# Retention attention and ELU FFN in one kernel: w_out staged and cast by GpSimd, first FFN1 tiles beside the last unit, the tail of batch 0 behind batch 1's units

## The chip, the cores and the metric

The kernel runs on one core of one Trainium2 chip. The metric is the device time of one execution in microseconds; a kernel is timed in several executions beside runs of the kernel before on the same chip. Each run comes with its span and its mean granted TensorE clock and is called fast or slow. PE is the matrix engine, PEld its weight load, DVE VectorE, ACT ScalarE, POOL GpSimd, SP SyncE, whose queue issues most transfers.

## The reference

```python
# q, k, v: (8, 8, 576, 64) fp32;  w_in: (512, 2048), w_out: (2048, 512) fp32
scores = scale * q @ k.T                       # per batch and head
D = gamma[h] ** (i - j)  where i >= j, else 0
x = ((scores * D) @ v)                         # -> (4608 tokens, 512)
h = x @ w_in
g = where(h > 0, h, exp(min(h, 0)) - 1)        # ELU
out = g @ w_out                                # (4608, 512) fp32
```

## The kernel before

A "unit" is a piece of attention: two 128-token chunks of four heads, or a tail of 64 tokens of all heads. A batch has four units and a tail, so units 0 to 3 and tail 4 are batch 0, units 5 to 8 and tail 9 batch 1. A unit is loaded in fp32, multiplied by decay factors into bf16 ("cast"), transposed (early units on PE, later ones by DMA), and then its matmuls run (`stretch`). The running state of a head group goes through `s_mid` and `s_end`, both made on GpSimd. The FFN works on blocks of 256 tokens: FFN1 tile (block, f) makes `ph`, the ELU makes `g`, FFN2 adds up in `pm`. All instructions are pinned: each engine runs its own in the order of the program.

Names in the lines below: `rqk`, `rv` are loaded q/k and v, `qkn`, `vn` their casts (`rqt`, `qkt`, `rvt`, `vt` for a tail), `ptr` a tile transposed on PE and `qkT` its copy (its "eviction") that the unit's matmuls read; `x`, `xt` are the attention result and its bf16 copy; `e` and `em` are exp(h) and exp(h) - 1 of the ELU; `ot` is the output copied out of `pm`. FT is 4 and NU is 5. Fillers are matmuls on zeros that only keep PE busy.

```python
def load_out(n):                               # w_out: cast fp32 -> bf16 in the transfer
    f = slice(n * 4, n * 4 + 4)
    pin(nc.gpsimd.dma_start(w_out_sb[:, f], moe_w_out.rearrange(...)[:, f]))

def cast(u, q="p", v="p"):                     # a full unit
    if q:
        cast_q(u, nc.vector if q == "v" else nc.gpsimd)   # two multiplies of q
        cast_q(u, nc.gpsimd, 1)                           # two multiplies of k
    if v:
        cast_v(u, v)

def stretch(u, quick=False):                   # cut: conditions
    new_x(); inter(u - 1); scores(u); values(u - 1); state(u)
    prefix_mid(u); put_mid(u)                  # DVE; POOL: s_mid
    masks(u)                                   # DVE, 1.2 us
    put_x(u - 1)                               # ACT
    prefix_end(u); put_end(u)                  # DVE; POOL: s_end

# ... end of the first stage
for ft in range(8, 16):
    ffn2(0, 0, [ft]); ffn2(0, 1, [ft], ps_x, "x0")
    if ft == 9:  cast(FT); cast(FT + 1, "v", "s")
    if ft == 11: load_to(FT + 7)
    if ft == 13: cast(FT + 2, "v", "s")
# second stage: q = FFN2 group of block 1, t = transposes, u = unit, f = FFN1 tile of block 2
for what in "q t q u t q u7 q t q u8 t q q u f t q f u f f t f9 u f f f".replace(" ", ""):
    if what == "7":   cast(FT + 3, "v", "s")
    elif what == "8": cast(FT + 4, "v", "s"); cast(FT + 5)
    elif what == "9": cast_later(FT + 6); cast_later(FT + 7); load_to(FT + 8)
    else: ...          # do it; after an "f" also chore(2): two pending casts
# main loop: FFN1 of block k beside FFN2 of block k - 1, a unit every few tiles
```

## Time and profile before

| | before |
|---|---|
| median (3 runs) | 326.02 us (325.49 to 326.57) |
| span of the profiled run | 324.5 us, clock 0.989 |
| end of the first FFN2 (last pm matmul before the ot copies) | 46.28 us |
| main loop starts (FFN1 tile (3,0)) | 72.11 us |
| last matmul ends | 319.68 us |

The last rows are read from the PE timeline. From 72 us on PE is full, so I read the kernel as a prologue and a main loop of 247.6 us (PE busy 243.5). The prediction below shows the lines.

### The profile page before, as it was taken

How to read it: one execution, taken by the hardware profiler on the slowest of the kernel's cores; microseconds unless marked ns; L12 is line 12 of the kernel's file. 1: busy time of each engine (PE TensorE's matmuls, PEld its weight loads, DVE VectorE, ACT ScalarE, POOL GpSimd, SP SyncE). 2: the span in 40 equal slices, each digit the busy share in tenths (PEclk: the TensorE clock that was granted, in tenths of full speed). 3: DMA queues.
4: the chain of work that ended last, by engine and by line, in shares of the span. 5: the costliest groups of instructions: out<-in, count | busy, mean ns of one | idle time of the engine just before them, and what ended most of it. 6: DMA issues, size and time to landing. Idle time of an engine off the chain costs nothing.

```text
span 324.5 us, 8896 instructions
## 1 busy us (share of the span) xinstructions
PE 304.5 (94%) x3566; PEld 205.8 (63%) x3610; DVE 205.9 (63%) x357; ACT 180.2 (56%) x352; POOL 168.1 (52%) x292
## 2 busy tenths in 40 slices
PE   7888989879899999999999999999999999999983
PEld 2347746666666676666676666667666667666641
DVE  3837756677577677667776767568666766555430
ACT  3527655585555565555665555655565555654531
POOL 5962414596777676846664857664593722010000
PEclk9959999999999999999999999999999999999999
DMA  7999999439999957966568496837685410001102
GB/s 208 259 177 205 229 274 222 120 67 259 260 211 200 229 133 161 228 162 162 149 164 203 107 245 151 171 119 188 157 148 130 73 45 35 32 34 48 49 33 66
DMA packets 99373, 49.60 MB, mean 153 GB/s; under 512 B 43588, under 2 KB 96836, under 8 KB 99332
## 3 DMA queue, kind: packets, MB, share of 16 engines
q1 hardware_dynamic: 92436, 36.19, 50.7%
q0 software_dynamic: 6896, 12.85, 16.5%
q8 instruction: 28, 0.46, 0.6%
q14 instruction: 13, 0.11, 0.1%
HBM read 36.70 MB, written 9.44 MB: 142 GB/s over the span
## 4 chain that ended last, share of the span: by engine, by line
PE 79%; DMA 7%; ACT 4%; DVE 3%; POOL 3%; issue 2%; SPq 1%; DVEq 0%; ACTq 0%; POOLq 0%
PE ph L65 35%; PE pm L65 35%; PE x L65 5%; PE sc L65 3%; DMA w_out_sb<-in_moe_w_out_dram 3%; DMA qkT<-qkn 2%; DMA rqk<-in_k_dram 2%; POOL qkn L186 1%; DVE g L505 1%; DVE g L509 1%; ACT xt L355 1%; ACT e L502 1%; ACT ot L520 1%; ACT ph L504 1%; SPq L175 1%
## 5 line engine op out<-in xcount | busy, mean ns | idle before, releaser
L65 PE MATMUL pm<-w_out_sb,g 128*128 128x512 bf16 x534 | 139.2, 379 | 4.1 <-ACT ot L520 1.7
L65 PE MATMUL ph<-xt,w_in_sb 128*128 128x256 bf16 x1024 | 134.0, 275 | 4.6 <-DVE g L509 2.3
L65 PEld LDWEIGHTS <-w_in_sb 128*128 128x128 bf16 x1152 | 110.5, 98 | 41.0 <-issue 6.1
L502 ACT ACTIVATE e<-ph 128x512 f32<-128x512 f32 x144 | 85.8, 597 | 88.6 <-PE ph L65 88.5
L65 PEld LDWEIGHTS <-g 128*128 128x128 bf16 x576 | 55.9, 98 | 44.5 <-issue 3.1
L505 DVE SCALAR_TENSOR_TENSOR g<-e,ph 128x512 bf16<-128x512 f32 x72 | 49.4, 686 | 43.4 <-ACT ph L504 42.3
L508 DVE TENSOR_SCALAR em<-e 128x512 bf16<-128x512 f32 x72 | 40.7, 565 | 33.3 <-ACT e L502 33.3
L381 POOL TENSOR_TENSOR s_mid<-mid,diag 128x256 bf16<-128x256 f32 x32 | 19.5, 611 | 75.3 <-DVE mid L390 39.6
L509 DVE SCALAR_TENSOR_TENSOR g<-ph,em 128x512 bf16<-128x512 f32 x72 | 49.8, 692 | 8.2 <-PE ph L65 0.9
L186 POOL TENSOR_TENSOR qkn<-rqk,gk 128x256 bf16<-128x256 f32 x64 | 40.6, 650 | 9.7 <-DMA rqk<-in_k_dram 9.5
L504 ACT ACTIVATE ph<-ph 128x512 f32<-128x512 f32 x72 | 42.7, 593 | 0.0
L536 POOL DMA_DIRECT2D out_dram<-ot x31 | 17.7, 573 | 40.0 <-ACT ot L520 39.9
L306 DVE TENSOR_TENSOR pt<-sc,mask 128x1024 bf16<-128x1024 f32 x31 | 37.7, 1216 | 0.4 <-PE sc L65 0.4
L355 ACT CAST xt<-x 128x256 bf16<-128x256 f32 x62 | 23.5, 450 | 24.5 <-PE x L65 20.5
L186 POOL TENSOR_TENSOR qkn<-rqk,gq 128x256 bf16<-128x256 f32 x48 | 30.8, 656 | 0.1
L520 ACT COPY ot<-pm 128x512 f32<-128x512 f32 x36 | 21.2, 590 | 7.0 <-PE pm L65 7.0
L381 POOL TENSOR_TENSOR s_end<-end,diag 128x256 bf16<-128x256 f32 x32 | 22.2, 696 | 2.1 <-DVE end L397 2.1
L65 PE MATMUL sc<-qkT 64*64 64x128 bf16 (+1 forms) x576 | 16.0, 220 | 1.4 <-DMA qkT<-qkn 0.8
L65 PE MATMUL ph<-xtt,w_in_sb 128*128 128x256 bf16 x128 | 16.6, 273 | 0.1
L231 POOL CAST vn<-rv 128x512 bf16<-128x512 f32 x25 | 16.2, 647 | 0.0
L65 PEld LDWEIGHTS <-qkT 64*64 64x64 bf16 x576 | 9.9, 106 | 6.7 <-ACT qkT L256 2.7
L256 ACT COPY qkT<-ptr 128x512 bf16<-128x512 bf16 x16 | 9.1, 596 | 8.3 <-PE ptr L255 8.3
(69 smaller groups left out, 166.8 us busy)
## 6 DMA issues: line engine op xcount, KB each, us to landing
rqk<-in_q_dram SPq DMA_DIRECT2D x32, 256.0 KB, 4.4
rqk<-in_k_dram SPq DMA_DIRECT2D x32, 256.0 KB, 4.2
rv<-in_v_dram SPq DMA_DIRECT2D x32, 256.0 KB, 5.0
out_dram<-ot POOLq DMA_DIRECT2D x31, 256.0 KB, 3.3
w_in_sb<-in_moe_w_in_dram POOLq DMA_DIRECT2D x4, 512.0 KB, 7.4
w_out_sb<-in_moe_w_out_dram POOLq DMA_DIRECT2D x4, 512.0 KB, 9.4
rqt<-in_q_dram SPq DMA_DIRECT2D x8, 128.0 KB, 3.8
rqt<-in_k_dram SPq DMA_DIRECT2D x8, 128.0 KB, 3.9
```

The lines of the kernel that those rows point to most:

```text
L65: pin(nc.tensor.matmul(*a, **kw))
L186: pin(eng.tensor_tensor(natt[u][0][:, i, e], x[:, e], g[:, e], ALU.mult))
L306: pin(nc.vector.tensor_tensor(pt.rearrange("p i h n -> p (i h) n"), sc.rearrange("p i (h n) -> p (i h) n", h=2), mask.rearrange("p k e r - ...
L355: pin(engines[eng[c]](dst.rearrange("p h (r e) -> p h e r", e=2), src))
L381: pin(eng.tensor_tensor(dst.rearrange("p h (j d) -> p h j d", j=2), src.unsqueeze(2).to_broadcast([P, 2, 2, D]), diag.unsqueeze(1).unsquee ...
L502: pin(nc.scalar.activation(e, ph, AF.Exp))
L504: pin(nc.scalar.activation(ph, ph, AF.Relu))
L505: pin(nc.vector.scalar_tensor_tensor(g, e, -1.0, ph, ALU.add, ALU.min))
L508: pin(nc.vector.tensor_scalar_add(em, e, -1.0))
L509: pin(nc.vector.scalar_tensor_tensor(g, ph, 0.0, em, ALU.max, ALU.min))
L520: pin(nc.scalar.copy(ot, pm))
L536: pin(eng.dma_start(out[r : r + P, :], ot))
```

## The change

Its intent: take the cast of w_out out of its transfers (they become plain loads from SP with casts on GpSimd), let the first FFN1 tiles fill PE while the last unit of batch 0 is prepared, and move tail 4 behind units 5 to 8. The core of the diff, with cuts (some arguments of calls too are cut):

```diff
-    def load_out(n):  # cast in the transfer, from GpSimd
+    def load_out(n):
+        staged[n] = raw.tile(...)
+        for i in range(2):
+            pin(nc.sync.dma_start(staged[n][:, i], moe_w_out[f * P : (f + 1) * P, :]))
+    def cast_out(n, eng="pp"):
+        for i in range(2):
+            pin(engines[eng[i]](w_out_sb[:, 2 * n + i], staged[n][:, i]))
...
+    sequence = [0, 1, 2, 3, 5, 6, 7, 8, 4] + list(range(9, NS))
...
+    turn_pe(3, "sv", 3, st[1])          # three filler matmuls
+    cast_v(3, "s")
+    ph = hidden(0, 0)                   # FFN1 tile (0,0) beside unit 3
...
+    ffn1(1, 0)
+    after(gts[1, 0], nc.sync)           # w_out is released here
+    for n in range(NFT // 2):
+        load_out(n)
+        cast_out(n)
+    load_to(NU + 1)                     # units 5, 6, 7 behind w_out
...
-    for what in "q t q u t q u7 q t q u8 t q q u f t q f u f f t f9 u f f f".replace(" ", ""):
+    for what in "q q q t q u t q u 7 q q t q u 8 f f t f u 4 f t f u 9 f t f u f".replace(" ", ""):
         if what == "7":
-            cast(FT + 3, "v", "s")
+            cast(NU + 2, "p", "s")      # q of unit 7 now on GpSimd
+            load_to(NU + 3)
         elif what == "8":
+            cast(NU + 3, "p", "s")
...
+        elif what == "4":
+            cast(FT)                    # tail of batch 0
+        elif what == "9":
+            cast(NU + FT)
...
+    for u in range(2 * NU, 2 * NU + 3):
+        cast_later(u)                   # units 10, 11, 12: only now
```

More of the change, by code (lines that the diff above doesn't have):

```diff
@@ L123 @@
     s_mid = [const.tile([P, 2, P], BF16, name=f"s_mid{w}") for w in range(2)]
-    s_end = [[const.tile([P, 2, P], BF16, name=f"s_end{w}{t}") for t in range(2)] for w in range(2)]
+    s_end = [[[const.tile([P, 2, P], BF16, name=f"s_end{w}{t}{o}") for o in range(2)] for t in range(2)]
+             for w in range(2)]
     diag = const.tile([P, 2], FP32, name="diag")
@@ L135, with load_in @@
     dummy = const.tile([1, 4], FP32, name="dummy")
-    def load_in(n):
-        c = slice(n * 512, (n + 1) * 512)
+    staged = {}
+    def load_in(a, b):
+        c = slice(a * 512, b * 512)
         pin(nc.gpsimd.dma_start(w_in_sb[:, :, c], moe_w_in.rearrange("(j p) c -> p j c", p=P)[:, :, c]))
     def load_out(n):
-        f = slice(n * 4, n * 4 + 4)
-        pin(nc.gpsimd.dma_start(w_out_sb[:, f], moe_w_out.rearrange("(f p) c -> p f c", p=P)[:, f]))
+        staged[n] = raw.tile([P, 2, 4, 2, D], FP32, name="rqk", tag="rqk").rearrange("p i h e d -> p i (h e d)")
+        for i in range(2):
+            f = 2 * n + i
+            pin(nc.sync.dma_start(staged[n][:, i], moe_w_out[f * P : (f + 1) * P, :]))
+    def cast_out(n, eng="pp"):
+        for i in range(2):
+            pin(engines[eng[i]](w_out_sb[:, 2 * n + i], staged[n][:, i]))
     def after(tile, eng):
@@ L244, in turn, with turn_pe @@
             pin(nc.sync.dma_start_transpose(trt[u], flat(u)))
-    def turn_pe(u, eng="vs", between=0):
+    def turn_pe(u, eng="vs", between=0, d=None):
         n = turn_tile(u)
@@ L249, in turn_pe @@
             if i and between:
-                warm(between)
+                warm(between, d)
             if i * 4 < n:
@@ L316, in inter @@
                 o = xps[0][:, hp * ST : (hp + 1) * ST]
-                acc_x(0, 2, o, s_end[hp // 2][1][:, hp % 2], trt[u][:, hp, :ST])
+                acc_x(0, 2, o, s_end[hp // 2][1][b % 2][:, hp % 2], trt[u][:, hp, :ST])
             return
@@ L321, in inter @@
                 continue
-            s = s_mid[w] if c else s_end[w][0]
+            s = s_mid[w] if c else s_end[w][0][b % 2]
             x = (to or xps)[c]
@@ L404, in put_end, with mask_half @@
         b, T, w, tail = unit(u)
-        block_diag(s_end[w][T], total[w])
-    def last_of_start(u, bank):
-        sc = score_ps.pop(u)
-        pt = ppool.tile([P, 2, 2, 2 * P], BF16, name="pt", tag="pt")
-        ptt[u] = pt
-        for hl in range(2):
-            pin(nc.vector.tensor_tensor(
-                pt[:, :, hl], sc.rearrange("p i (h n) -> p i h n", h=2)[:, :, hl],
-                mask.rearrange("p k e r -> p (k e r)").unsqueeze(1).to_broadcast([P, 2, 2 * P]), ALU.mult,
-            ))
-        first = [hidden(0, 0)]
-        for hl in range(2):
-            values(u, (hl,), bank)
-            inter(u, (hl,), bank)
-            put_x(u, (hl,), bank, ("ss", "sv")[hl])
-            if hl == 0:
-                first.append(hidden(0, 1, ps_m, "pm"))
-        drop(u)
-        elu(0, 0, first[0])
-        elu(0, 1, first[1])
+        block_diag(s_end[w][T][b % 2], total[w])
+    def mask_half(u, hl):
+        if hl == 0:
+            ptt[u] = ppool.tile([P, 2, 2, 2 * P], BF16, name="pt", tag="pt")
+        pin(nc.vector.tensor_tensor(
+            ptt[u][:, :, hl], score_ps[u].rearrange("p i (h n) -> p i h n", h=2)[:, :, hl],
+            mask.rearrange("p k e r -> p (k e r)").unsqueeze(1).to_broadcast([P, 2, 2 * P]), ALU.mult,
+        ))
+    before = [None]
     def stretch(u, quick=False):
-        late = u - 1 in natt and u - 1 in ptt
+        p, before[0] = before[0], u
+        late = p is not None
         carry = u < NS and not unit(u)[3]
@@ L433, in stretch @@
         if late:
-            inter(u - 1)
+            inter(p)
         if u < NS:
@@ L437, in stretch @@
         if late:
-            values(u - 1)
+            values(p)
         if carry:
@@ L444, in stretch @@
         if late and not quick:
-            put_x(u - 1)
+            put_x(p)
         if u < NS:
@@ L449, in stretch @@
             if quick:
-                put_x(u - 1)
-            drop(u - 1)
+                put_x(p)
+            drop(p)
         if carry:
@@ L457, in stretch @@
             put_end(u)
-    def finish(u):
-        new_x()
-        inter(u)
-        values(u)
-        put_x(u)
-        drop(u)
     xts, gts, acc = {}, {}, {}
@@ L496, in hidden, with elu, elu_act @@
         return ph
-    def elu(k, f, ph):
-        relu = f % 2 == 1
+    def elu(k, f, ph, relu=None):
+        elu_act(k, f, ph, relu)()
+    def elu_act(k, f, ph, relu=None):
+        relu = f % 2 == 1 if relu is None else relu
         e = epool.tile([P, TG], FP32, name="e", tag="e")
@@ L504, in elu, with rest @@
             pin(nc.scalar.activation(ph, ph, AF.Relu))
-            pin(nc.vector.scalar_tensor_tensor(g, e, -1.0, ph, ALU.add, ALU.min))
-        else:
-            em = epool.tile([P, TG], BF16, name="em", tag="em")
-            pin(nc.vector.tensor_scalar_add(em, e, -1.0))
-            pin(nc.vector.scalar_tensor_tensor(g, ph, 0.0, em, ALU.max, ALU.min))
+        def rest():
+            if relu:
+                pin(nc.vector.scalar_tensor_tensor(g, e, -1.0, ph, ALU.add, ALU.min))
+            else:
+                em = epool.tile([P, TG], BF16, name="em", tag="em")
+                pin(nc.vector.tensor_scalar_add(em, e, -1.0))
+                pin(nc.vector.scalar_tensor_tensor(g, ph, 0.0, em, ALU.max, ALU.min))
+        return rest
     def ffn2(k, it, fts, pool=None, tag="pm"):
@@ L548, with load_to @@
     loaded = [0]
-    def load_to(u):
-        while loaded[0] <= u:
-            load(loaded[0], last=(loaded[0] == FT - 1))
+    sequence = [0, 1, 2, 3, 5, 6, 7, 8, 4] + list(range(9, NS))
+    def load_to(n):
+        while loaded[0] <= min(n, NS - 1):
+            load(sequence[loaded[0]], last=(loaded[0] == FT - 1))
             loaded[0] += 1
@@ L561 @@
     cast(1, "v", None)
-    load_in(0)
+    load_in(0, 1)
     for u in range(FT - 1):
@@ L581 @@
             cast(2, "v", None)
-            load_in(1)
             warm(2, st[1])
@@ L591 @@
             put_end(1)
+            load_in(1, 2)
             cast_q(3, nc.vector)
             cast_q(3, nc.gpsimd, 1)
-            cast_v(3, "p")
-            load_in(2)
-            load_in(3)
             warm(3, st[1])
-    masks(2)
-    turn_pe(3, "vs")
-    st3 = [ps_h.tile([P, TG], FP32, name="st", tag="ph") for _ in range(2)]
-    state(3, st3)
     prefix_mid(2)
@@ L604 @@
     prefix_end(2)
+    load_in(2, 4)
+    masks(2)
+    turn_pe(3, "sv", 3, st[1])
+    cast_v(3, "s")
+    ph = hidden(0, 0)
+    st3 = [ps_h.tile([P, TG], FP32, name="st", tag="ph") for _ in range(2)]
+    state(3, st3)
     prefix_mid(3)
@@ L608 @@
     scores(3)
+    rest = elu_act(0, 0, ph, True)
+    mask_half(3, 0)
+    rest()
+    mask_half(3, 1)
+    ph = hidden(0, 1, ps_m, "pm")
     new_x()
@@ L613 @@
     drop(2)
-    last_of_start(3, st3)
+    elu(0, 1, ph)
     put_end(2)
     put_end(3)
-    load_out(0)
-    after(s_end[0][1].rearrange("p h d -> p (h d)"), nc.sync)
-    load_to(FT + 3)
-    for blk, n in ((1, 0), (0, 1), (1, 1)):
-        ffn1(blk, 2 * n)
-        ffn1(blk, 2 * n + 1)
-        after(gts[blk, 2 * n], nc.gpsimd)
-        load_out({(1, 0): 1, (0, 1): 2, (1, 1): 3}[blk, n])
+    for hl in range(2):
+        values(3, (hl,), st3)
+        inter(3, (hl,), st3)
+        put_x(3, (hl,), st3, ("ss", "sv")[hl])
+        if hl == 0:
+            ffn1(0, 2)
+    drop(3)
+    ffn1(1, 0)
[4 more added lines that the diff above has]
+    load_to(NU + 1)
+    ffn1(0, 3)
+    for f in range(1, 4):
+        ffn1(1, f)
     for n in range(2, 4):
@@ L632 @@
         ffn2(0, 1, [ft], ps_x, "x0")
-        if ft == 9:
-            cast(FT)
-            cast(FT + 1, "v", "s")
-        if ft == 11:
-            load_to(FT + 7)
-        if ft == 13:
-            cast(FT + 2, "v", "s")
-    turns = [lambda u=u: turn_pe(u, "ss") for u in range(FT, NU + FT + 1)]
-    units = [lambda u=u: stretch(u, True) for u in range(FT, NU + FT + 1)]
+    cast(NU, "v", "s")
+    cast(NU + 1, "v", "s")
+    order = sequence[4:10]
+    turns = [lambda u=u: turn_pe(u, "ss") for u in order]
+    units = [lambda u=u: stretch(u, True) for u in order]
     quads = [lambda it=it, part=part: ffn2(1, it, part) for it in range(2) for part in Q]
     tiles = [lambda f=f: ffn1(2, f) for f in range(8)]
-    for what in "q t q u t q u7 q t q u8 t q q u f t q f u f f t f9 u f f f".replace(" ", ""):
+    for what in "q q q t q u t q u 7 q q t q u 8 f f t f u 4 f t f u 9 f t f u f".replace(" ", ""):
         if what == "7":
-            cast(FT + 3, "v", "s")
+            cast(NU + 2, "p", "s")
+            load_to(NU + 3)
         elif what == "8":
-            cast(FT + 4, "v", "s")
-            cast(FT + 5)
+            cast(NU + 3, "p", "s")
+            load_to(NU + 4)
+        elif what == "4":
+            cast(FT)
+            load_to(NU + 5)
         elif what == "9":
-            cast_later(FT + 6)
-            cast_later(FT + 7)
-            load_to(FT + 8)
+            cast(NU + FT)
+            load_to(NU + 6)
         else:
             {"q": quads, "t": turns, "u": units, "f": tiles}[what].pop(0)()
-            if what == "f":
-                chore(2)
     assert not (turns or units or quads or tiles)
-    cast_later(FT + 8)
-    load_to(FT + 10)
     stores()
-    first = FT + 6
+    for u in range(2 * NU, 2 * NU + 3):
+        cast_later(u)
+        load_to(u + 2)
+    first = 2 * NU
     slots = {}
```

## The prediction

> **What bounds the kernel now.** I read the page first, for where the matmul engine is full.
>
> ```profile
> PE   7888989879899999999999999999999999999983
> ...
> PEclk9959999999999999999999999999999999999999
> DMA  7999999439999957966568496837685410001102
> ```
>
> One slice is 8.1 us. From about 72 us to the end PE stands at 9: the rest is the fixed FFN work at full clock and nothing in the diff makes it smaller. Anything to win or lose lies in the first nine slices. There PE has holes, the clock dips in slice 3, and the transfer engines are full for seven slices. The table by stretches puts sizes on this:
>
> ```profile
> 45.60:72.10 26.50, 22.21 (x368) 15.73 (x370) 15.79 (x29) 17.12 (x37) 14.63 (x24) 1.00 0.67 149
> 72.10:100.00 27.90, 26.29 (x347) 18.34 (x352) 20.47 (x33) 15.72 (x31) 19.20 (x33) 1.00 1.13 245
> 0.00:25.26 25.26, 19.74 (x269) 9.65 (x272) 13.21 (x41) 10.04 (x23) 17.47 (x43) 0.86 1.03 213
> ```
>
> The first figure after the stretch's length is PE busy, then PEld, DVE, ACT, POOL, then the clock. PE is idle 5.5 us up to 25.3, and loses 3.3 us more there to a half clock (0.50 from 18.0 to about 24.5: 6.5 us at half speed). From 45.6 to 72.1 it is idle 4.3 us. With 1.5 us between these, some 14.5 us are lost before the main loop starts at 72.1 (first tile of FFN block 3). That is the whole purse: a gain of 2% (6.5 us) must take nearly half of it.
>
> Next, the waits of PE over the whole span and the POOL timeline:
>
> ```profile
> PE ph L65 <- DVE g L509: 2.3, 2, 1.7
> PE ph L65 <- ACT xt L355: 1.8, 3, 0.9
> PE pm L65 <- ACT ot L520: 1.7, 3, 0.8
> ...
> PE pm L65 <- DMA w_out_sb<-in_moe_w_out_dram: 0.4, 1, 0.4
> ```
>
> The w_out transfers, which the chain view charges with 3% (10.85 us), make PE wait only 0.4 us. They land just in time, at 44.4. Taking the cast out of them can give 0.4 us directly.
>
> ```profile
> 51.72 0.61 POOL L381 TENSOR_TENSOR s_mid<-mid,diag 128x256 bf16<-128x256 f32 x1 [6.47 <-DVE mid L390]
> 53.05 0.73 POOL L381 TENSOR_TENSOR s_end<-end,diag 128x256 bf16<-128x256 f32 x1 [0.72 <-DVE end L397]
> 53.74 1.36 POOL L186 TENSOR_TENSOR qkn<-rqk,gk 128x256 bf16<-128x256 f32 x2
> ```
>
> POOL works in program order. Unit 5's state matmuls end at 51.2; s_end is done at 53.8, because DVE's mask (1.2 us) lies between. So a cast written after a unit starts on POOL 2.55 us after that unit's last matmul. Unit 6 shows it again: 54.9 to 57.5. Before, this cost PE nothing, since casts run two units ahead: unit 8's k cast ends at 58.8, its transposes start at 60.3.
>
> **What the Trainium skill says.** "DMA: Bandwidth & Descriptors", Issuing engines are not separate DMA queues: transfers from SP and POOL share the same 16 engines. The trace agrees: the DMA share is 1.06 to 1.24 from 5 to 60 us whichever queue issues, so moving w_out to SP makes no bandwidth. Same page, Rules for kernel authors: a cast during a DMA is issued from GpSimd; so w_out from SP must be cast by an engine. "GPSIMD Engine Reference", 4.1 Engine selection: one-input elementwise work is roughly at line rate on GpSimd, two-input work about 2x slower than on VectorE. Here the 128x512 cast takes 647 ns on POOL, a 128x256 two-input multiply 656 ns, against a median of 426 ns on DVE: 1.5x. "TensorE: Matmul & The Clock Gate", Why this matters for your kernels: PE-idle gaps above about 3 us bring the half clock back. The trace has the half clock at 18 us after a stretch of short matmuls (1.23 us busy in 15 to 17), without a single gap of 3 us; the 1.7 us gap at 65.7 did not cause it.
>
> **The change, part by part.**
>
> (a) *Start, to FFN1 tile (1,0), at 25.26 before.* POOL loses the vn cast of unit 3 (0.6) and gets one w_in issue fewer; tile (0,0) is issued while unit 3 is prepared; three filler matmuls are added. By rows: w_in's first quarter is issued at 9.4 and lands in up to 8.3 us, at 17.7; tile (0,0) at full clock 0.95 to 18.7; state and scores 0.7; tile (0,1) 0.9; unit 2's matmuls 0.9 to 21.2. Then ACT is in the way: xt of unit 2 (0.76), exp and relu of tile 1 (1.1), xt (0.5), exp of tile 2 (0.6), then DVE em, g, xt (1.5): 25.7. So three tiles done by 25.8, where before has two by 25.3 and three by 26.2: gain 0.4 us. The half clock goes (3.3 us), but most of this turns into waiting for that chain.
>
> (b) *w_out to the end of FFN2 of half block 0, at 45.6 before.* SP waits for g of tile (1,0): matmuls to 26.7, exp, em, g about 1.9: 28.6. The dummy transfer takes 0.76 to issue; first 256 KB lands some 2.9 later (the shortest landing of a 256 KB load): 32.3; cast 0.65: 33.0. PE wants it at 31.4 (five tiles from 25.8 at about 1.05, as before's seven took 7.35, and one more): 1.6 us wait. Then 16 slices of 262 KB at 270 to 310 GB/s of what is read (estimates: 20.8 to 44.4 us before carried some 6.4 MB; 5 to 10 us ran at 295) take 0.85 to 0.97 us each, beside a 0.65 us cast that hides. The last is ready at 45.5 to 47.5. FFN2 ends near 46.7: **loss 1.1 us**. The 16 casts (10.4 us of POOL) fill its idle time.
>
> (c) *Second stage, 26.5 us before.* The loads of units 5 to 8 now follow w_out, so k of unit 7 lands about 52.7, and casts run only one unit ahead; q of units 7 and 8 is now on POOL: four multiplies, 2.44 us. Unit 7: two matmul groups (1.75) after unit 6, its transposes come up; POOL is at 2.55 + 2.44 = 5.0, transposes end at 5.3. They take 0.6 themselves, so PE idles 2.95. Unit 8: two FFN tiles follow unit 7 (the known 0.9 xt wait, done at 2.95): idle 1.75. Unit 4, the moved tail: its cast stands behind unit 8's s_end, late by the ELU of the tile before (about 3.3), 1.2 more, one tile (0.9) to cover it: idle 3.5. Unit 9's cast is hidden. With the 0.45 for ot and 0.4 in evictions the stage idles 0.45 + 0.4 + 2.95 + 0.9 + 1.75 + 3.5 = 10 us instead of 4.3: with rounding **loss 5.7 to 7 us**; I take 6.5.
>
> (d) *Main loop.* Before, unit 10's casts were slipped in from "f9" on; now they come after the tail casts and four output issues (2.2): about 12.3 us after unit 8's end, plus some 4.2 for the DMA transpose: 16.5. PE is at unit 10 after 10.5 + 3.5 = 14. Idle 2.2, against 0.8 before at unit 11: loss 1.4. The rest is unchanged.
>
> Sum: -0.4 + 1.1 + 6.5 + 1.4 = +8.6 us: 326.0 + 8.6 = **334.6 us**.
>
> **The rivals.** First, the clock: without the half clock 3.3 us come back in full, w_out at 310 GB/s lands by 44.5, the stalls of (c) are shorter since PE arrives later: about 328 to 330, same. For it: the fillers and early tiles clearly aim there. Against: the ACT chain of (a), each piece of which has a measured row. Second, the clock the other way: stalls of 3 us bring the half clock back in the second stage, 1 to 2 us each: 337 to 341. For it: the dip at 18 us; against: 1.7 us at 65.7 did nothing. Third, transfers become the bound: if w_out runs below 270 GB/s, units 7 and 8 land after POOL could cast them, and (b) and (c) grow by 2 to 4 us. For it: landings of up to 13.5 us under load; against: w_out's rows are 2 KB, units' pieces 512 B. Fourth, a real gain: all waits of (c) hidden and the clock kept, some 320. I see nothing that hides them.
>
> **Range and chances.** 334.5 us. The stalls in (c) follow from program order and measured durations, so a loss is likelier than not; that (a) and (b) give 3 to 4 us more than I count is quite possible. 8 in 10: 328 to 341. The 2% lines are 319.5 and 332.5. Faster 0.06 (half the purse would have to be won), same 0.32, slower 0.62.
>
> **What would show it.** (a) clock 1.00 from 15 to 26, PE waiting for ACT xt near 24 and tile (1,0) at 25.8; (b) first w_out matmul near 33, a wait for a POOL cast there, last near 46.7; (c) PE "ptr" waits for POOL qkn and qkt of about 3, 1.7 and 3.5 us between 55 and 76; (d) main loop starting near 80 and a wait of about 2 us for a qkT transfer just after. The prediction is wrong if the main loop starts at or before 74, which needs POOL's casts ahead of PE, or if the loop itself runs at another rate than its 247.6 us from 72.1 to 319.7.

## The result, and the profile after

The changed kernel takes 338.28 us in the median of four runs (334.36, 339.77, 338.86, 337.7; the second counts as slow, at a clock of 0.971; the median of the three fast ones is 337.7), the kernel before 326.19 us beside it. The ratio is 1.0333, 95% interval 1.0241 to 1.0425: slower. A ratio here is the mean time of one kernel's fast runs over that of the other's of the same rounds, so it isn't quite the ratio of the medians that I quote. The profiled run is the fastest, 334.36 us (span 332.7); what follows is read from it, and it therefore shows 8.2 of the 12.1 us by which the medians differ.

First the same rows of the page, in 40 slices of 8.3 us.

```profile
PE   8778986757999999999999999999999999999994
...
PEclk9999999799999999999999999999999999999999
DMA  7994999927589995895856885856569410000102
```

The clock dip has moved from slice 3 to slice 8, PE is now at 6, 7, 5 and 7 tenths in slices 7 to 10 (9, 8, 7 and 9 before), and the transfer engines now have a hole in the fourth slice, where SP waits to release w_out. The table by stretches (PE, PEld, DVE, ACT, POOL busy, clock, DMA share, GB/s):

```profile
0.00:25.10 25.10, 20.07 (x287) 10.50 (x288) 15.12 (x45) 12.79 (x28) 15.05 (x40) 1.00 0.98 209
25.10:45.00 19.90, 18.31 (x132) 12.72 (x131) 12.37 (x21) 11.22 (x21) 10.13 (x16) 1.00 0.82 265
45.00:79.30 34.30, 24.68 (x368) 15.94 (x368) 14.42 (x26) 18.48 (x37) 19.04 (x33) 0.95 0.90 210
```

The second stage, 25.8 us before (46.28 to 72.11), lasts 34.3 us: PE idles 9.6 us of it, where it idled 4.3 in the prediction's stretch of before. The clock of 0.95 over 34.3 us is another 1.7 us. The PE waits of the whole run:

```profile
PE ptr L264 <- POOL qkn L195: 4.4, 12, 1.3
PE ptr L264 <- POOL qkt L207: 3.1, 2, 2.8
PE ph L65 <- DVE g L508: 2.3, 3, 1.8
PE ph L65 <- ACT xt L364: 1.8, 3, 0.9
PE pm L65 <- POOL w_out_sb L152: 1.4, 1, 1.4
```

The first two are the stalls of step (c), but for 1.2 us of `qkn` waits in the first stage: transposes ("ptr") that wait for multiplies on GpSimd. Here is one transpose before (unit 8, no wait), and the first of unit 7 after:

```profile
60.30 0.61 PE L255 MATMUL ptr<-ident,qkn 128*128 128x128 bf16 x8
57.00 0.28 PE L264 MATMUL ptr<-ident,qkn 128*128 128x128 bf16 x2 [1.26 <-POOL qkn L195]
```

The timelines of PE and POOL around tail 4 show the order that makes the longest one:

```profile
69.02 1.05 PE L65 MATMUL ph<-xt,w_in_sb 128*128 128x256 bf16 x8
72.91 0.28 PE L264 MATMUL ptr<-ident,qkt 128*128 128x128 bf16 x2 [2.84 <-POOL qkt L207]
```

```profile
71.67 0.61 POOL L390 TENSOR_TENSOR s_end<-end,diag 128x256 bf16<-128x256 f32 x1 [0.65 <-DVE end L406]
72.24 1.19 POOL L207 TENSOR_TENSOR qkt<-rqt,gq 128x256 bf16<-128x256 f32 x2
```

POOL was idle before 71.67 and tail 4's data had long landed (its loads were issued by 52.5 us, and no load of a tail takes more than 5.9 us to land); but its cast stands behind unit 8's s_end in the program, and s_end waits for DVE. PE had one tile to do meanwhile.

One thing nobody foretold stands at the start of the main loop (DVE timeline):

```profile
78.56 3.61 DVE L507 TENSOR_SCALAR em<-e 128x512 bf16<-128x512 f32 x1 [0.35 <-ACT e L498]
82.27 0.69 DVE L508 SCALAR_TENSOR_TENSOR g<-ph,em 128x512 bf16<-128x512 f32 x1
```

An em takes 0.46 us in the median; this one took 3.61, and PE waited 1.81 us for its g.

| | before | after | difference |
|---|---|---|---|
| nine FFN1 tiles done | 32.6 | 30.3 | -2.3 |
| end of the first FFN2 | 46.28 | 44.99 | -1.3 |
| main loop starts | 72.11 | 79.3 | +7.2 |
| last matmul ends | 319.68 | 327.97 | +8.3 |

The second stage thus costs 8.5 us, the main loop 1.1 more, and the start had won 1.3.

### The profile page after: what moved, and what is told of

Its sections match the earlier page's. It is cut to its first block, busy times and chain, and to the rows that moved or that the text cites. A ratio compares the mean times of both kernels' runs of the same rounds, so it can differ in the third digit from the quotient of the medians.

```text
span 332.7 us, 8976 instructions
## 1 busy us (share of the span) xinstructions
PE 308.6 (93%) x3613; PEld 205.7 (62%) x3613; DVE 204.9 (62%) x352; ACT 181.8 (55%) x354; POOL 174.8 (53%) x303
## 4 chain that ended last, share of the span: by engine, by line
PE 77%; DMA 7%; POOL 5%; DVE 4%; ACT 3%; SPq 2%; issue 2%; DVEq 0%; POOLq 0%; ACTq 0%
PE pm L65 34%; PE ph L65 34%; PE x L65 5%; PE sc L65 3%; DMA rqk<-in_moe_w_out_dram 3%; POOL qkn L195 2%; DMA rv<-in_v_dram 2%; DMA rqk<-in_k_dram 2%; DVE em L507 1%; SPq L184 1%; ACT e L498 1%; DVE g L508 1%; POOL s_end L390 1%; SPq L148 1%; POOL s_mid L390 1%
## 5 line engine op out<-in xcount | busy, mean ns | idle before, releaser
L65 PE MATMUL pm<-w_out_sb,g 128*128 128x512 bf16 x576 | 147.0, 380 | 2.7 <-POOL w_out_sb L152 1.4
L65 PE MATMUL ph<-xt,w_in_sb 128*128 128x256 bf16 x1024 | 132.6, 273 | 4.7 <-DVE g L508 2.3
L504 DVE SCALAR_TENSOR_TENSOR g<-e,ph 128x512 bf16<-128x512 f32 x73 | 50.2, 687 | 44.6 <-ACT ph L500 43.6
L507 DVE TENSOR_SCALAR em<-e 128x512 bf16<-128x512 f32 x71 | 42.9, 604 | 38.0 <-ACT e L498 38.0
L508 DVE SCALAR_TENSOR_TENSOR g<-ph,em 128x512 bf16<-128x512 f32 x71 | 49.1, 691 | 7.8 <-PE ph L65 0.5
L195 POOL TENSOR_TENSOR qkn<-rqk,gk 128x256 bf16<-128x256 f32 x64 | 39.7, 638 | 7.1 <-DMA rqk<-in_k_dram 6.9
L195 POOL TENSOR_TENSOR qkn<-rqk,gq 128x256 bf16<-128x256 f32 x52 | 33.4, 658 | 0.1
L152 POOL CAST w_out_sb<-rqk 128x512 bf16<-128x512 f32 x16 | 10.1, 641 | 13.0 <-DMA rqk<-in_moe_w_out_dram 12.4
```

Source lines behind the costliest of these rows:

```text
L65: pin(nc.tensor.matmul(*a, **kw))
L195: pin(eng.tensor_tensor(natt[u][0][:, i, e], x[:, e], g[:, e], ALU.mult))
L504: pin(nc.vector.scalar_tensor_tensor(g, e, -1.0, ph, ALU.add, ALU.min))
L507: pin(nc.vector.tensor_scalar_add(em, e, -1.0))
L508: pin(nc.vector.scalar_tensor_tensor(g, ph, 0.0, em, ALU.max, ALU.min))
```

## The experiments

Eleven kernels ran (e2 twice), all with right results.

### e1: q of units 7 and 8 back on VectorE

```diff
-            cast(NU + 2, "p", "s")
+            cast(NU + 2, "v", "s")
-            cast(NU + 3, "p", "s")
+            cast(NU + 3, "v", "s")
```

> The changed kernel with one edit: the q multiplies of units 7 and 8 go to VectorE instead of GpSimd. Theory A (transposes of units 7, 8 and 4 wait because their casts stand on GpSimd behind the preceding unit's s_end): two of four multiplies (1.2 us) leave GpSimd for each of the two units, so the transpose waits on qkn between 55 and 68 us fall from 3.2 us to about 1, the main loop starts some 2.4 us sooner, and the half clock at 57 to 61 us may go too: 334 to 336 against 338. Rival B (the loads behind w_out come too late): same waits, now ended by transfers, 338.

Measured: 331.6, 331.42, 338.2 and 338.62 us (before: 326.35); the last two are slow, at clocks of 0.98. The PE waits from 45 to 85 us have POOL qkn at 0.5 and DVE qkn at 0.8 us instead of POOL qkn at 3.2; the tail's wait (3.1 us) is untouched. The waits go as theory A says, and no transfer took their place; a wait of 1.3 us for a g did, and the half clock only moved, to 71.5 us. The fast runs lie below the 334 to 336 us expected. By how much the time falls is inconclusive: two fast runs, and the changed kernel's own fast runs spread over 4.5 us.

### e2 and e2b: the casts one unit earlier

```diff
-"q q q t q u t q u 7 q q t q u 8 f f t f u 4 f t f u 9 f t f u f"
+"q q q t q u 7 t q u 8 q q t q u 4 f f t f u 9 f t f u f t f u f"
```

> The changed kernel with the casts (and loads) of units 7, 8, 4 and 9 each written one unit earlier, as far ahead as in the kernel before; engines unchanged. Theory A: the transpose waits on qkn and qkt (6.3 us in the second stage) fall below 1 us, the half clock there goes, the second stage shrinks from 34.3 to about 27 us, total 329 to 331. Rival B: GpSimd now waits for the transfers of units 7 and 8 instead, later s_mid and s_end are held up behind them, and less than 2 us are won: 336 or more.

> The same kernel as e2_casts_ahead, whose only profile fell in a run of 1735 us and shows nothing. Theory A, which its times (330 to 331) favoured: in the second stage the transpose waits on GpSimd multiplies stay below 1 us in sum and the clock stays at 1.00; 330 to 331 again. Rival B: waits for transfers in their place.

Measured: 330.85, 330.21, 330.88 us (ratio 1.0137), then 330.28, 327.75, 330.74, 329.45 us on another chip (ratio 1.0089). One run of e2, the profiled one, took 1736 us; I have no explanation for it and read nothing from it, hence e2b. In e2b's PE waits from 45 to 90 us no wait on a GpSimd multiply is left at all; the first lines are

```profile
PE ph L65 <- DVE g L508: 2.8, 2, 2.5
PE ptr L264 <- DVE g L508: 1.1, 1, 1.1
PE ph L65 <- ACT xt L364: 0.9, 1, 0.9
```

So theory A holds: moving the four places where casts and loads are issued, with no work taken away, removes 6.3 us of waits and brings the ratio from 1.0333 to 1.0137 and 1.0089 (the mean of the fast runs from 337 to 330 us). Rival B is out for this order: the data were there. The longest wait left, 2.5 us, is for the g behind a long em again (4.38 us from 72.04 on), and a half clock follows it (0.74 in 75 to 80 us), against the expectation.

### e3: the second stage of before behind the new start and the staging

Against the changed kernel, with cuts:

```diff
-sequence = [0, 1, 2, 3, 5, 6, 7, 8, 4] + list(range(9, NS))
+sequence = list(range(NS))
     for ft in range(8, 16):
...
+        if ft == 9:  cast(FT); cast(FT + 1, "v", "s")
+        if ft == 11: load_to(FT + 7)
+        if ft == 13: cast(FT + 2, "v", "s")
...
-"q q q t q u t q u 7 q q t q u 8 f f t f u 4 f t f u 9 f t f u f"
+"q t q u t q u7 q t q u8 t q q u f t q f u f f t f9 u f f f"     # with before's casts at 7, 8, 9
```

> The changed kernel's start and staged w_out, with the second stage of the kernel before (tail first, its order of tiles, casts two units ahead, early casts for the main loop). Theory A: the whole loss lies in the second stage; that stage takes about 26 us again and the 1.3 us that start and staging had won by the end of the first FFN2 remain: 324 to 326. Rival B (staging moves the loads of units 4 to 7 behind w_out and these then come too late for any order): waits for transfers of 3 us or more after 45 us, 329 or more.

Measured: 334.13 us, ratio 1.0242. Theory A in this form is a miss. The PE timeline shows where the time went:

```profile
44.69 0.59 PE L65 MATMUL pm<-w_out_sb,g 128*128 128x512 bf16 x2 [0.39 <-POOL w_out_sb L152]
52.16 1.86 PE L65 MATMUL pm<-w_out_sb,g 128*128 128x512 bf16 x4 [6.88 <-ACT ot L521]
```

The old stage has v casts on ACT ahead of the ot copies. With the loads of units 4 to 6 behind w_out, ACT waits there for data (6.48 us before the first v cast, 2.04 before the second), and the ot copy behind it:

```profile
51.01 0.62 ACT L240 CAST vn<-rv 128x512 bf16<-128x512 f32 x1 [2.04 <-DMA rv<-in_v_dram]
```

Rival B is right in part: staging on SP does make the units late, and the old order cannot bear it.

### e4: the new start alone

Against e3, with cuts:

```diff
-    after(gts[1, 0], nc.sync)
-    for n in range(NFT // 2):
-        load_out(n)
-        cast_out(n)
+    load_out(0)                          # right after unit 3's s_end, as in before
+    after(s_end[0][1][0], nc.sync)       # (its first row)
+    load_to(FT + 3)
...
+    load_out(1)                          # after tile (1,0); 2 and 3 after two more tiles each
```

> The new start alone (first FFN1 tiles beside unit 3, fillers), with w_out cast in its transfers and the second stage of the kernel before. Theory A: no half clock from 18 to 24 us and tile (1,0) near 24 instead of 25.3 with one more tile done, so about 1.5 to 2 us less: 324 to 325. Rival C (the w_out landing at 44 us sets the end of the first FFN2 whatever comes before it): PE waits 2 us more for w_out, total 326 as before.

Measured: 326.5 us, ratio 1.0026 (interval 0.9975 to 1.0077): same. The time is as rival C said, but not quite for its reason: it named the last w_out landing, at 44 us, and in the profiled run (329.52, the slowest of four) PE waits 2.44 us for the first transfer, at 33 us, and 1.96 us for an ot copy, which stands on ACT behind a v cast that waits for its load:

```profile
33.37 0.59 PE L65 MATMUL pm<-w_out_sb,g 128*128 128x512 bf16 x2 [2.44 <-DMA w_out_sb<-in_moe_w_out_dram]
...
48.51 1.25 PE L65 MATMUL pm<-w_out_sb,g 128*128 128x512 bf16 x4 [1.96 <-ACT ot L515]
```

What the start wins is given back at the next waits. e3 against e4 also shows that staging with the units' loads put behind w_out, under the old order, costs 7.6 us by the medians; the two edits were not run apart.

### e5: the early casts behind the ot copies

Against e3:

```diff
-        if ft == 9:
-            cast(FT); cast(FT + 1, "v", "s")
-        if ft == 11: load_to(FT + 7)
-        if ft == 13: cast(FT + 2, "v", "s")
+    cast(FT); cast(FT + 1, "v", "s"); load_to(FT + 7); cast(FT + 2, "v", "s")
```

> e3_old_second_stage with one edit: the early casts of units 4, 5 and 6 stand behind the two ot copies. In e3 PE waited 6.9 us for an ot copy. Theory D (ScalarE works in program order and the v cast of unit 6, written ahead of the ot copies, waits for its late transfer): the 6.9 us wait becomes under 0.6, total 326 to 328, with a smaller wait for late units after it. Rival B in its strong form (the units come too late for any order): the same 6 us turn up as waits of the transposes or of s_mid, total 332 or more.

Measured: 331.69 us, ratio 1.0155 (e3: 1.0242). The 6.9 us wait for ot becomes 0.7 in sum, as theory D says; but a wait of 3.8 us for a transposed tile's eviction on ACT has taken its place, and the clock is at 0.56 from 50 to 55 us. Between the two theories, and above theory D's 326 to 328: the order on ACT set where the late data hurt, and some 60% of the loss against before (4.7 of 7.8 us) stays.

### e6 and e9: is it the long em?

Tiles of the named blocks use the other ELU form, which has no em:

```diff
-        elu(k, f, hidden(k, f))
+        elu(k, f, hidden(k, f), True if (k, f) in ((2, 6), (3, 0)) else None)                     # e6
+        elu(k, f, hidden(k, f), True if (k, f) in ((2, 4), (2, 6), (3, 0), (3, 2)) else None)     # e9
```

> The changed kernel, where the ELU of two tiles (block 2 tile 6, block 3 tile 0) goes by the relu form, which has no em instruction. In the changed kernel's trace one em lasted 3.61 us instead of 0.43 while GpSimd ran multiplies without a break, and PE waited 1.81 us for it at the start of the main loop. Theory E (em cannot get at SBUF while GpSimd reads and writes it; the other forms can): no VectorE instruction over 1.5 us between 74 and 90 us, and that wait is gone or under 0.5 us. Rival F (VectorE is slow there for any instruction, or em waited for its input): the relu form's g is stretched likewise and the wait stays.

> The changed kernel with tiles 4 and 6 of block 2 and 0 and 2 of block 3 in the relu form, so that no em stands beside GpSimd's unbroken stretch of work from 70 to 84 us. In e6, with two such tiles, the em before them took the stall: 5.84 us from 74.3 on. Theory E (em cannot get at SBUF until GpSimd leaves a gap): no VectorE instruction above 1.5 us between 68 and 90 us, no PE wait on g above 0.6 us there, 1.8 to 4 us less than the changed kernel: 333 to 336. Rival F (VectorE stalls there whatever it runs): another instruction is stretched to several us and the time stays at 334 to 339.

e6 ran once, 339.43 us at a clock of 0.978 (a single run, state unknown). It missed its aim in a telling way: the em of the tile before, untouched by the edit, met the same work on POOL.

```profile
74.34 5.84 DVE L507 TENSOR_SCALAR em<-e 128x512 bf16<-128x512 f32 x1 [3.59 <-ACT e L498]
```

```profile
73.64 2.23 POOL L537 DMA_DIRECT2D out_dram<-ot  x4
75.89 1.19 POOL L195 TENSOR_TENSOR qkn<-rqk,gk 128x256 bf16<-128x256 f32 x2
77.03 1.18 POOL L195 TENSOR_TENSOR qkn<-rqk,gq 128x256 bf16<-128x256 f32 x2
78.15 0.60 POOL L240 CAST vn<-rv 128x512 bf16<-128x512 f32 x1
78.72 1.17 POOL L195 TENSOR_TENSOR qkn<-rqk,gk 128x256 bf16<-128x256 f32 x2
79.86 1.35 POOL L195 TENSOR_TENSOR qkn<-rqk,gq 128x256 bf16<-128x256 f32 x2
```

em ends at 80.18, just where POOL's pair takes 1.35 us instead of 1.18: I read this as em getting in there while POOL waited. Before that, each POOL instruction starts a little before the end of the one ahead (0.57 us apart, 0.60 long). The same pairing stands in the changed kernel and in e2b.

e9 takes all such em away: 334.25 us median (333.13 to 334.6), ratio 1.0235. No DVE instruction between 68 and 90 us is longer than 1.22 us, and the PE wait on g is gone; rival F is out. Against the changed kernel's profiled run that is 2 us of wait removed, but no clear gain against its fastest run (334.36). The clock differs, though: e9's profiled run has a second half clock,

```profile
71.46:78.28 6.82, 5.84 (x53) 4.22 (x54) 1.90 (x3) 2.71 (x6) 6.80 (x13) 0.50 0.47 141
```

which that run doesn't have and which costs some 3.4 us (an estimate: half of 6.8), and all four runs of e9 have a lower mean clock (0.979 to 0.988) than the changed kernel's fast ones (0.990 to 0.993). So e9 shows that the long em and its wait go, but not what they cost in whole time. The other two fast runs of the changed kernel (338.86 and 337.7) are higher than any of e9's four; they have no trace, so whether the em stall makes that spread isn't shown.

### e11: a burst of GpSimd work in the kernel before

The set-up of the unused tiles is cut.

```diff
+            if (blk, f) == (NB - 2, 4):
+                after(gts[blk, f], nc.gpsimd)
+                for _ in range(12):
+                    pin(nc.gpsimd.tensor_tensor(b_dst, b_src, b_src, ALU.mult))
```

> The kernel before with twelve back-to-back GpSimd multiplies of unused data (128x256, some 0.61 us each, 7.3 us in all), released by a g near 297 us, where GpSimd is otherwise idle and PE full. Results are unchanged. Theory E (an em that meets unbroken GpSimd work waits until it ends): one em near 297 to 306 us lasts 2 to 7 us, PE waits for g there 1 to 5 us, and the time rises by as much: 327.5 to 331. Rival F (em and GpSimd do not exclude each other; the long em had another cause): no em above 1 us there, 326.

Measured: 325.98, 326.59, 325.82 us in fast runs, ratio 0.9995: nothing. The profiled run was slow (449.46 us, clock 0.657), so only its DVE and POOL order can be read. There the em inside the burst took 0.53 us. The burst is not the one of e6, though: its twelve multiplies write one tile, and each starts 0.69 us after the last at a length of 0.61, so there is a gap of 0.08 us between them. So "busy POOL" is not enough to hold em up, and theory E as I wrote it for this run fell. What remains is narrower: the long em stand beside POOL work without gaps. The same trace has such a place, outside the burst: an em of 2.59 us at 35.02, while POOL runs five instructions, each starting before the end of the one ahead. Why em is let in at the one place and not earlier stays open.

### e7, e8 and e10: a version that beats both

e7 is e2 with three edits (cut: some later `load_to` and `cast_later` calls, which move with the third):

```diff
     mask_half(3, 1)
+    after(gts[0, 0], nc.sync)           # w_out released at tile (0,0), not (1,0)
+    for n in range(NFT // 2):
+        load_out(n)
...
-            cast(NU + 2, "p", "s")      # and the same for NU + 3
+            cast(NU + 2, "v", "s")
...
         elif what == "9":
             cast(NU + FT)
+            cast_later(2 * NU)
...
+            if what == "f":
+                chore(2)
```

> e2_casts_ahead with three edits meant to give a version that beats both: w_out's transfers are released by g of tile (0,0) at 21 us instead of tile (1,0) at 27; q of units 7 and 8 on VectorE; unit 10's casts spread over the last four tiles of the second stage. Theory A with B's remainder: the idle transfer engines at 25 to 30 us are used, the 1.4 us wait for w_out goes, units 5 to 9 land some 5 us sooner; main loop starts near 69 to 71, total 322 to 325. If the early w_out only slows w_in: a wait for w_in of 1 us or more near 22 to 30 us and 327 or more.

Measured: 332.73 us, ratio 1.0186, where 322 to 325 was expected. The prologue went as meant: no wait for w_out, main loop from about 70.4 us. Then PE waited 6.57 us for unit 11's DMA transpose. The SP timeline shows why: the loads of units 12 to 14 had come to stand behind unit 10's transpose, and unit 11's behind them.

```profile
69.72 1.36 SPq L253 DMA_TRANSPOSE qkT<-qkn  x1
...
80.52 0.83 SPq L178 DMA_DIRECT2D rvt<-in_v_dram  x1
81.94 2.09 SPq L253 DMA_TRANSPOSE qkT<-qkn  x1
```

e8 moves the loads up, as far as unit 14 (cut: the later calls of `load_to` in e7 fall away):

```diff
             cast(NU + FT)
+            load_to(2 * NU + 4)         # loads up to unit 14 before unit 10's transpose
             cast_later(2 * NU)
-            load_to(NU + 6)
```

> e7_w_out_earlier with one edit: the loads of units 11 to 14 are issued before unit 10's DMA transpose instead of behind it. In e7 the first units and w_out came early as meant (main loop from 70.4 us against 72.1 in the kernel before), but the transpose of unit 11 was issued at 81.9 behind loads of units 12 to 14 that had themselves stood behind unit 10's transpose, and PE waited 6.6 us for it. Theory G (SyncE works in program order): that wait falls below 1 us, main loop from about 70.4 us, total 323.5 to 325.5. Rival H (the transpose is late because of its casts on GpSimd): the wait stays above 3 us, 328 or more.

Measured over five runs: 322.88 us (322.5 to 323.59), before 326.32, ratio 0.9888, interval 0.9869 to 0.9906: 1.1% faster, clear of noise but under the 2% line. The wait for the transpose is gone, as theory G says; the clock row of its page shows 9 in every slice. Stretches near the ones above (w_out now moves from 26 us on):

```profile
26.00:31.00 5.00, 4.80 (x42) 3.98 (x41) 3.60 (x6) 4.34 (x9) 3.04 (x5) 1.00 1.06 400
31.00:45.00 14.00, 13.44 (x90) 8.72 (x91) 9.90 (x17) 7.99 (x16) 9.43 (x16) 1.00 1.14 330
45.00:70.00 25.00, 20.83 (x360) 14.94 (x361) 15.19 (x27) 16.82 (x35) 13.97 (x23) 1.00 0.86 204
```

e10 is e8 with w_out cast in its transfers again, so without the staging of the change's title:

```diff
-    after(gts[0, 0], nc.sync)
-    for n in range(NFT // 2):
-        load_out(n)                      # staged, from SP
...
-    for n in range(NFT // 2):
-        cast_out(n)
+    for n in range(4):
+        load_out(n)                      # cast in the transfer, from GpSimd, after unit 3's s_end
+    after(gts[1, 0], nc.sync)            # then the units
     load_to(NU + 1)
```

> e8_loads_before_transpose with w_out cast in its transfers again (four transfers from GpSimd right after unit 3's s_end, no staging, no casts), units from tile (1,0)'s g on. If staging as such is worth something (theory I: the 2 KB rows of the staged loads move faster, 345 to 390 GB/s of fp32 in 31 to 45 us, and w_out comes in sixteen pieces as PE needs them), PE waits 1 us or more for w_out near 31 to 44 us and for units after it: 324 to 327. If staging is neutral (rival K: same fp32 bytes through the same engines): within 1 us of 322.9.

Measured: 322.9 us, ratio 0.9906 (interval 0.9847 to 0.9965; one run of before took 398 us and is slow): the same as e8. Rival K holds: no worth of staging as such is seen here. What the two have in common is the start, the tail behind batch 1's units, and an order in which no engine's next instruction waits long for something late. The start alone won nothing (e4); the place of the tail was never changed alone, so its share isn't shown.

## Why the prediction was right

Total, direction and main mechanism were right: 334.5 us foretold, in a range of 328 to 341, 338.28 measured. By its own steps, on the profiled run:

- **(a) Start.** The half clock at 18 us went, and the ACT chain did make PE wait for xt, as foretold. The gain was mis-sized: 0.4 us foretold (at three tiles), 2.3 us measured at nine tiles done (30.3 against 32.6). The term that failed is the chain of ACT and DVE after tile 2: I set its end at 25.7, it ended at 24.75; and three matmuls of tile (1,0) ran at 23.7 without waiting for its end, the rest from 24.8.
- **(b) w_out.** The wait for the first slice was foretold at 1.6 us and measured at 1.39. That this is near is luck: my sum was off (six tiles of 1.05 from 25.8 end at 32.1, not 31.4, so 0.9 us of wait), and both PE and the slice came earlier than I had them. The rest was too dear: I had the last slice ready at 45.5 to 47.5, the last cast ended at 44.26. Most of that is the start: the first slice was ready at 31.7, not 33.0. From there to the last took 12.6 us, where I had 12.5 to 14.5, so the rate was at the fast end of my 270 to 310 GB/s (fifteen slices of 262 KB in 12.6 us are 313). And I had misread the kernel before: its first FFN2 ends at 46.28, not at 45.6. So this step with (a) is a gain of 1.3 us, not a loss of 0.7.
- **(c) Second stage.** This carried the loss, as foretold. Idle was foretold at 10 us and is 9.6. Singly: unit 7, 2.95 foretold and 2.1 measured; unit 8, 1.75 and 1.05; tail 4, 3.5 and 3.1; an eviction wait at unit 5 made up for the rest, 1.1 us where I had 0.4 for all. The 1.7 us that the half clock took, the second rival, came on top. Foretold 6.5 in sum, measured 8.5: 5.3 more idle (9.6 against 4.3), 1.7 of clock, 0.7 because I began the stage at 45.6, and the rest longer PE work. e2 and e2b test the mechanism itself: with the casts one unit earlier these waits vanish.
- **(d) Main loop.** The size was near (1.4 foretold, 1.1 measured), the mechanism was wrong. I expected unit 10 to wait for its DMA transpose; it did not. PE waited 1.81 us for a g behind the long em instead, which no step of mine had, although it is the same crowding of late casts on POOL that I had counted. "SBUF — State Buffer" of the Trainium skill, section Who interferes with whom, would have let me see the danger: it says that GpSimd shares a port pair with VectorE, that `tensor_scalar` can enter a mode that needs it, and that the one that issues first keeps the pair for the whole instruction. em is a tensor_scalar; that it ran in that mode no trace shows. The traces agree in kind (3.61, 4.38 and 5.84 us for an undisturbed 0.43), but not in length, as below.

On the clock: "TensorE: Matmul & The Clock Gate", Part 1, gives a free-running window of 3413 ns after which the clock changes. The dip fits it: 0.83 in each of the two stretches of 5 us from 55 to 65 is 2 x 0.17 x 5 = 1.7 us lost, or 3.4 us at half clock. The trace has

```profile
58.29:61.70 3.41, 3.13 (x38) 1.69 (x40) 0.00 (x0) 1.36 (x3) 0.37 (x1) 0.50 1.21 289
```

and in the other traces too a half clock lasts one such window or two (3.41 us in e1, 6.82 us before and in e9), but for those at the end of a run. It came after waits of which none exceeded 1.3 us, while the single wait of 2.84 us at 70 us brought none. It isn't so in every run: the same wait of 2.84 us for tail 4 stands in e1, e6 and e9, and there the clock goes to half in or soon after it, from 71.5, 70.3 and 71.5 us on. In the 3.41 us before that PE was busy 1.08, 1.22 and 1.37 us. In the changed kernel's trace, windows of 3.41 us counted on from 58.29 cut the wait in two, at 71.94, and have PE busy 1.54 and 2.15 us. So where a wait falls in the window differs between runs. A limit of busy time does not come out: the window ahead of the dip at 58.29 has 1.57 us (0.72 of it transposes), more than the 1.54 that brought none.

Of the rivals, the one I gave for "same" (full gain of the clock, w_out early) was right in part: w_out was in by 44.3, the start won 2.3 of the 3.3 us, the stalls were somewhat shorter; the second stage ate it. The second rival, the clock, was right that the stage loses 1.7 us to it, in e9 more.

That the sum came out near is partly luck: (a) with (b) came out 2.0 us better than foretold and (c) 2.0 us worse. And the steps are checked on the fastest run alone; the other two fast runs are 3.3 and 4.5 us longer, and what they lose stays open. Two readings in the prediction are loose: its "1.5x" sets a mean on POOL beside a median on DVE (by medians 610 to 426 ns, 1.4x), and the DMA share in 55 to 60 us is 1.04, not 1.06.

## What to carry to other kernels

When engines run in program order, a cheap instruction costs what stands ahead of it in its queue: before moving work to an idle engine, or later in a program, ask what that engine will be waiting for when the data are ready, and put the work ahead of that wait if the data have landed, behind it if they have not (e2 and e5 are the two sides of this). Saved waiting in a prologue is only worth something if the next wait down the line moves too; e4 won nothing, e8, which changes the later stages too, won 1.1% with the same start. Spread late chores on GpSimd rather than running them off in one piece beside VectorE (in e8, which spreads unit 10's casts, the longest em is 1.89 us, not 3.61).

## What the Trainium skill lacked or had wrong

- "SBUF — State Buffer", Who interferes with whom, says that the pair is held for one whole instruction. In these runs em stayed blocked across several GpSimd instructions in a row, 3.61, 4.38 and 5.84 us against a length of 0.43 us, and it got in beside neighbours 0.08 us apart with a delay of 0.1 us (e11). The page says nothing of who gets the pair next when work is queued on both sides; what decides it is open here too.
- "TensorE: Matmul & The Clock Gate", Why this matters for your kernels, warns of idle gaps above about 3 us. Here a half clock came after many short waits (none over 1.3 us ahead of the dip at 58 us), and after one wait of 2.84 us it came in e1, e6 and e9 and stayed away in the changed kernel. The window of Part 1 fits better than the rule, and a later section there, on a second failure mode, does report clock drops from frequent short idling; what no section gives is how busy a window must be: 1.57 us of 3.41 brought a half clock, 1.54 did not.
- "DMA: Bandwidth & Descriptors", Rules for kernel authors, names GpSimd for casts in a transfer but gives no price for it against a plain load and a cast by an engine. In e8 and e10 both give the same time, 322.88 and 322.90 us.
- No page that I found warns of the position of a transpose among loads in SP's queue: 6.57 us in e7, none in e8.
